# Attention outputs with tokens on partitions, in a fused attention and mixture-of-experts kernel

## The chip, the cores and the metric

One core of a Trainium2 chip runs the whole program. The metric is the device time of one execution in microseconds; lower is better. All arithmetic is float32 (some matmuls of the expert part in a rounded float32 form).

## What is computed

The reference chains three parts: a linear attention with a complex decay for each position and row, a top-1 mixture of experts with a skip test, and a second feed-forward layer. Cut to what matters here:

```python
# q, k, v, a_re, a_im: (B, H, S, D) = (4, 8, 768, 48); a is normalised to magnitude at most 0.999
for t in range(S):
    S_re, S_im = ar * S_re - ai * S_im + k_t v_t^T, ar * S_im + ai * S_re
    y[:, :, t] = q_t^T S_re
x = y as (3072 tokens, 384)                 # heads side by side
skip = x @ w_skip > 0                       # only these tokens are computed
logits = x @ w_gate                         # 8 experts, the largest is taken
x += gate * (relu(x @ w1[e]) @ w2[e])       # on the computed tokens
out = max(x @ m1, x @ m2, x @ m3) @ m_out
```

w_gate and w_skip stand side by side as nine columns ("logits" below means all nine).

## The kernel before

**Two stages.** The attention turns the decays into running products and angles, so that q and k can be scaled and turned beforehand and a step becomes ordinary masked attention within 128 tokens (a chunk) and a state between chunks. Behind it the routing and the experts run; their instructions have line 49 in the profile, since they are issued through a recording helper.

**What sets the order.** Every operation is given to a planner (class Plan) with an engine, an assumed duration and the tiles it reads and writes. The planner walks through time with these durations, always takes the ready operation with the earliest place in the program shifted by a bias, and writes down a fixed order for each engine. The biases are in the table PRIO (by kind of operation and batch). Each engine then runs its order strictly.

**Preparing q and k.** For each batch (the last in two parts, so five units) and each of three groups of 128 rows, ScalarE (line 444) and VectorE (line 476) compute logarithms, angles and their sines in the tiles wa, wCD and wR and multiply q and k (wqk) with them; two scans on VectorE (lines 514 and 560) run along time. The last values of the scans are copied into rhoend and phend (lines 517 and 563, on VectorE). DMAs on SP's queue (line 571, the last unit's second half on GpSimd's) stack the results into qks, where each head has 48 rows of real and 48 of imaginary part; rows 96 to 127 are padding, zeroed by three DMAs (blank, line 325).

**A step** (function step) handles one chunk of one batch for four heads; 48 steps in all. Each half of the heads has its own single buffers, so that its steps follow each other through them:
- line 608: four transposes of k into the bank pk; ScalarE copies them to kn (line 610);
- line 621: scores, eight matmuls in which 64 keys at a time are stationary and the queries stream: 128 columns for the first 64 keys, 64 for the second (their upper triangle is left out). A float32 matmul is two records in the trace, so 16 records. The order alternates heads and halves of the partitions so that two equal widths stand side by side;
- line 624: VectorE multiplies the 256 columns on the diagonal with the mask into pt; line 627: ScalarE copies the other 128 columns;
- line 637: the state z is updated with kn stationary and v streaming in 64 columns; line 642: ScalarE copies it to st;
- line 652: outputs from the state, with st stationary and q streaming in 128 columns;
- line 659: outputs from the scores, v stationary in quarters of 64 x 64 and the scores streaming. v is needed on the other half of the partitions too, so half of it comes a second time in another arrangement (cross, from the array vx, two chunks a load, line 436, two buffers). The outputs stand with head dimensions on partitions;
- line 662: ScalarE copies the outputs to ysb; line 666, the picks: with ysb stationary, the tile w9p (an identity beside the nine weight columns) streams in 105 columns, which turns the outputs to tokens on partitions and appends the nine partial logits; lines 674 and 676: ScalarE copies both to xt and lgw; line 683 sums the logits, line 687 stores x (SP).

SP's queue carries, in one order, the loads of a, q and k (line 421), v (428), cross (436), the stacks (571), the stores of x (687) and later the expert weights. When the tiles of the preparation are no longer used, their memory goes to the expert weights (a mark named swap), whose loads then start.

## Time and profile before

| | us |
|---|---|
| runs: median (lowest to highest of 3) | 677.92 (675.98 to 678.57) |
| profiled execution, device time | 670.54 |
| its span, first to last instruction | 668.8 |
| TensorE busy | 592.6 (89%) |
| VectorE busy | 455.7 (68%) |
| ScalarE busy | 383.0 (57%) |
| GpSimd busy | 62.9 (9%) |

Busy time is the time in which an engine had an instruction running; matmuls overlap each other, so a busy TensorE can still take more work. A row of the timeline or of the chain begins with its start and its length in us. In rows by group, "idle before" is the engine's idle time ahead of these instructions and what ended it.

### The profile page before, as it was taken

How to read it: one execution, taken by the hardware profiler on the slowest of the kernel's cores; microseconds unless marked ns; L12 is line 12 of the kernel's file. 1: busy time of each engine (PE TensorE's matmuls, PEld its weight loads, DVE VectorE, ACT ScalarE, POOL GpSimd, SP SyncE). 2: the span in 40 equal slices, each digit the busy share in tenths (PEclk: the TensorE clock that was granted, in tenths of full speed). 3: DMA queues.
4: the chain of work that ended last, by engine and by line, in shares of the span. 5: the costliest groups of instructions: out<-in, count | busy, mean ns of one | idle time of the engine just before them, and what ended most of it. 6: DMA issues, size and time to landing. Idle time of an engine off the chain costs nothing.

```text
span 668.8 us, 14161 instructions
## 1 busy us (share of the span) xinstructions
PE 592.6 (89%) x5669; PEld 547.0 (82%) x5669; DVE 455.7 (68%) x748; ACT 383.0 (57%) x800; POOL 62.9 (9%) x73
## 2 busy tenths in 40 slices
PE   0008988999999999989999999999999999999996
PEld 0007877889888889979999999899898898998995
DVE  6997999989778766999999854837456464303120
ACT  7797999999967666667677422523324333213120
POOL 1000000000012021030100163204020000000000
PEclk9999999999999999999999999999999999999998
DMA  9979779978749667868884456344042140010000
GB/s 307 301 189 263 291 215 317 289 219 275 210 141 299 223 201 241 307 218 293 274 288 162 156 154 207 99 152 131 1 167 93 32 170 12 13 36 0 25 25 28
DMA packets 60025, 117.40 MB, mean 176 GB/s; under 512 B 6032, under 2 KB 45472, under 8 KB 59952
## 3 DMA queue, kind: packets, MB, share of 16 engines
q1 hardware_dynamic: 51584, 84.57, 40.5%
q10 hardware_dynamic: 4512, 19.66, 8.5%
q0 software_dynamic: 3856, 12.19, 6.2%
q8 instruction: 46, 0.75, 0.5%
q14 instruction: 27, 0.22, 0.1%
HBM read 82.59 MB, written 12.58 MB: 142 GB/s over the span
## 4 chain that ended last, share of the span: by engine, by line
PE 65%; DVE 11%; ACT 11%; DMA 6%; issue 4%; SPq 1%; POOL 0%; ACTq 0%; POOLq 0%; DVEq 0%
PE bank L49 56%; ACT wCD L444 4%; DVE wqk L476 2%; PE bank L659 2%; PE bank L621 2%; DVE wR L476 2%; ACT wa L444 2%; DVE u L49 2%; PE bank L637 1%; DMA w9p<-in_w 1%; DMA wraw<-y_slot,r_grow 1%; PE bank L666 1%; PE bank L652 1%; DMA x<-in_m 1%; ACT kn L610 1%
## 5 line engine op out<-in xcount | busy, mean ns | idle before, releaser
L49 PE MATMUL bank<-ar,wh 128*128 128x512 f32 (+1 forms) x504 | 137.2, 359 | 0.7 <-DVE xs L49 0.7
L49 PEld LDWEIGHTS bank<-ar,wh 128*128 128x128 f32 x504 | 90.0, 189 | 14.9 <-DVE xs L49 1.0
L49 PE MATMUL bank<-ar,wl 128*128 128x512 f32 (+1 forms) x252 | 90.5, 359 | 0.0
L49 DVE TENSOR_TENSOR xs<-bank,xs 128x512 f32<-128x512 f32 (+1 forms) x42 | 25.7, 613 | 69.9 <-PE bank L49 69.7
L608 PE MATMUL bank<-ident,qks 96*128 96x96 f32 x160 | 22.8, 269 | 52.3 <-DMA qks<-wqk 50.8
L49 PE MATMUL bank<-ar,sm 128*128 128x384 f32 x348 | 67.0, 337 | 0.0
L49 PE MATMUL bank<-xth,ar 128*128 128x256 f32 x312 | 63.4, 287 | 3.0 <-DVE sm L49 2.2
L608 PEld LDWEIGHTS bank<-ident,qks 96*128 96x128 f32 x160 | 15.5, 147 | 56.0 <-issue 45.4
L49 PEld LDWEIGHTS bank<-ar,sm 128*128 128x128 f32 x348 | 59.2, 189 | 0.0
L49 DVE TENSOR_TENSOR ar<-wraw,ar 128x768 fp32r<-128x768 f32 x58 | 54.6, 952 | 4.3 <-ACT ar L49 4.0
L49 PEld LDWEIGHTS bank<-xth,ar 128*128 128x128 f32 x312 | 50.9, 190 | 5.1 <-DVE sm L49 3.3
L49 ACT CAST ar<-wraw 128x768 fp32r<-128x768 f32 x58 | 48.2, 834 | 11.4 <-PE bank L49 8.5
L49 PE MATMUL bank<-woh,sm 128*128 128x384 f32 x192 | 53.9, 334 | 0.0
L49 ACT COPY ysb<-bank 128x384 f32<-128x384 f32 x40 | 18.6, 479 | 61.6 <-PE bank L49 61.3
L49 PEld LDWEIGHTS bank<-ar,wl 128*128 128x128 f32 x252 | 47.6, 189 | 6.9
L444 ACT ACTIVATE wCD<-wCD 128x768 f32<-128x768 f32 (+3 forms) x67 | 51.1, 790 | 2.7 <-DVE wCD L514 2.5
L621 PE MATMUL bank<-qks 128*64 128x128 f32 (+1 forms) x768 | 42.4, 254 | 3.2 <-ACT pt L627 1.8
L49 PE MATMUL bank<-xtl,ar 128*128 128x256 f32 x156 | 44.0, 282 | 0.0
L444 ACT ACTIVATE wa<-wa 128x768 f32<-128x768 int32 (+8 forms) x53 | 41.3, 801 | 3.3 <-DVE wa L560 2.3
L49 ACT ACTIVATE wraw<-wraw 128x768 f32<-128x768 f32 x24 | 19.6, 843 | 40.9 <-DVE u L49 35.1
L621 PEld LDWEIGHTS bank<-qks 128*64 128x64 f32 x768 | 38.5, 141 | 5.3 <-ACT pt L627 2.5
L49 PE MATMUL bank<-lnh,ar 128*128 128x384 f32 x144 | 40.9, 337 | 0.0
(223 smaller groups left out, 1411.7 us busy)
## 6 DMA issues: line engine op xcount, KB each, us to landing
wraw<-in_w SPq DMA_DIRECT2D x62, 384.0 KB, 4.8
wraw<-in_a ACTq DMA_DIRECT2D x12, 768.0 KB, 5.4
wqk<-in_qk SPq DMA_DIRECT2D x9, 768.0 KB, 9.5
x<-in_m ACTq DMA_DIRECT2D x9, 768.0 KB, 7.0
qks<-wR SPq DMA_DIRECT2D x18, 288.0 KB, 4.3
qks<-wqk SPq DMA_DIRECT2D x18, 288.0 KB, 5.2
v<-in_v SPq DMA_DIRECT2D x4, 1152.0 KB, 12.1
wa<-in_a SPq DMA_DIRECT2D x6, 768.0 KB, 13.4
```

Of the source, the lines that this page charges most:

```text
L49: return lambda *a, **kw: fn(*map(placed, a), **{n: placed(x) for n, x in kw.items()})
L444: lambda: nc.scalar.activation(out=out[0], in_=in_[0], func=f, **kw), keys(in_), keys(out))
L476: pl.add("DVE", t, lambda: fn(out=out[0], **{m: i[0] for m, i in zip(names, ins)}, **kw), keys(*ins), keys(out), bias=bias)
L608: nc.tensor.transpose(pk[:, h, :2 * D], K[:2 * D, h, sl], ident[:2 * D, :2 * D])
L610: pl.add("ACT", t_acp(384), lambda: nc.scalar.copy(kn[:, 0:8 * D].rearrange("p (h r) -> p h r", r=2 * D), pk[:, :, 0:2 * D]), (pkk,), (knk ...
L621: nc.tensor.matmul(p6[side[o], quads(j, n), :], K[:, 2 * j + o, part[n]], Q[:, 2 * j + o, part[n].start:sl.stop], start=True, stop=True)
L637: nc.tensor.matmul(z[side[o], h * ZW:h * ZW + ZW], kn[:, at:at + HC], vcols(h, ZW), start=c == 0 and h == 0, stop=c == NC - 2 and h == 3, ...
L652: nc.tensor.matmul(py[side[h % 2], h // 2, :], sp[0][:, h * D:h * D + 64], Q[:, h, sl], start=h < 2, stop=False, skip_group_check=True)
L659: nc.tensor.matmul(py[side[o], j, n * HC:], half(j, n, o), t6[side[o], quads(j, n), :], start=c == 0 and j + n == 0, stop=n == 1, skip_gro ...
L666: nc.tensor.matmul(px[side[o], j, :], ysb[:, j, side[o]], w9p[:, 2 * hh + j, :], start=True, stop=True)
```

## The change

The outputs are computed with tokens on partitions at once, so that the turn by the picks is not needed:
- Outputs from the scores: the masked scores are stationary (128 keys x 64 tokens) and v streams. Outputs from the state: q is stationary (64 tokens at a time) and the state streams. Each head streams 57 columns: 48 of v and 9 that hold v times the head's nine weight columns. The picks, ysb and the copy of outputs go; xt and lgw are copied straight from the outputs' bank.
- The nine columns of v: for each chunk the transposed v (array vt, 192 KB a chunk, tile vt with one buffer) is loaded, multiplied with the weights arranged by head (six matmuls of 72 columns, in the bank that also takes the transposes of k), and ScalarE copies the 72 columns into v's wider tile. The state carries the columns too (57 in place of 48).
- Scores: all four heads, one after the other, wide and narrow matmul in turn; the mask is 512 columns wide (128 a head) and the copy of unmasked scores goes. The part of the bank that no matmul writes is zeroed once.
- cross and vx go. The padding of qks is zeroed by GpSimd memsets at the start in place of DMAs.
- The copies to rhoend and phend move from VectorE to ScalarE.
- The table PRIO has new numbers, so the planner's order differs in many places; rows of it stand in the prediction.

```diff
-PRIO = dict(FE=(-150, 400, 200, -200, 400), FT=(400, 400, 100, 10, 200), AE=(10, -100, 60, 150, -200),
+PRIO = dict(FE=(-150, 300, 200, 250, 30), FT=(300, 400, 100, -30, 30), AE=(150, 30, 150, 250, 60), AT=(0, 150, -150, -30, -100),
...
-VW = HD // 2
-VG = 2
-XW = 2 * D + 9
+VW = D + 9
...
-    ring("pt", [P, 6 * HC], NPT)
-    ring("ysb", [P, 2, C], 2)
+    ring("vt", [P, KD, C], 1)
+    ring("pt", [P, 4 * C], NPT)
...
+    for t in qks:
+        nc.gpsimd.memset(t[2 * D:], 0.0)
...
+    def load_vt(b, c):
+        t, k = pl.take("vt")
+        pl.dma(lambda: nc.sync.dma_start(out=t, in_=vt[b, c].rearrange("p (k s) -> p k s", k=KD)), 5 * C * HD, (), (k,),
+               after=stacked.get(b - 1, ()))
+        return t, k
...
-        pl.add("DVE", 75, lambda: nc.vector.tensor_copy(out=rhoend[:, i:i + 1], in_=Dt[0][:, n - 1:n]), keys(Dt), (("rho", i),),
-               bias=PRIO["FE"][now[0]])
+        pl.add("ACT", 190, lambda: nc.scalar.copy(rhoend[:, i:i + 1], Dt[0][:, n - 1:n]), keys(Dt), (("rho", i),))
...
-        pl.add("DVE", 85, lambda: nc.vector.tensor_copy(out=phend[:, i, c0:c1], in_=c3(Bt[0])[:, :, C - 1]), keys(Bt), (("ph", i),),
-               bias=PRIO["FT"][now[0]])
+        pl.add("ACT", 195, lambda: nc.scalar.copy(phend[:, i, c0:c1], c3(Bt[0])[:, :, C - 1]), keys(Bt), (("ph", i),))
...
+        if hh == 0:
+            tv, tvk = load_vt(b, c)
+            lw = pk[:, 8 * D:8 * D + H * 9]
+
+            def f():
+                for k in range(KD):
+                    for o in range(2):
+                        nc.tensor.matmul(lw[side[o]], tv[:, k, side[o]], w9p[:, k, :], start=k == 0, stop=k == KD - 1,
+                                         skip_group_check=True)
+            pl.add("PE", 6 * 63, f, (tvk, "w9p"), (pkk,), form=1)
...
+        if hh == 0:
+            pl.add("ACT", t_acp(72), lambda: nc.scalar.copy(
+                vt[:, c * H * VW:(c + 1) * H * VW].rearrange("p (h w) -> p h w", w=VW)[:, :, D:],
+                lw.rearrange("p (h n) -> p h n", n=9)), (pkk,), vk[1:], bias=PRIO["kn"][b])
...
-            for j, n, o in heads:
-                nc.tensor.matmul(p6[side[o], quads(j, n), :], K[:, 2 * j + o, part[n]], Q[:, 2 * j + o, part[n].start:sl.stop],
-                                 start=True, stop=True)
+            for h in range(4):
+                for n in range(2):
+                    nc.tensor.matmul(p4[side[n], h, n * HC:], K[:, h, part[n]], Q[:, h, part[n].start:sl.stop], start=True, stop=True)
...
-        masked = pl.add("DVE", t_dve(4 * HC) + 10, lambda: nc.vector.tensor_tensor(
-            out=t6[:, 0:4], in0=p6[:, 0:4], in1=mask[:, None, :].to_broadcast([P, 4, HC]), op=ALU.mult), (ppk,), (ptk,),
+        masked = pl.add("DVE", t_dve(4 * C) + 10, lambda: nc.vector.tensor_tensor(
+            out=t4, in0=p4, in1=mask[:, None, :].to_broadcast([P, 4, C]), op=ALU.mult), (ppk,), (ptk,),
             bias=PRIO["mask"][b])
-        pl.add("ACT", t_acp(2 * HC), lambda: nc.scalar.copy(pt[:, 4 * HC:6 * HC], pp[:, 4 * HC:6 * HC]), (ppk,), (free,),
-               after=(masked,), bias=PRIO["free"][b])
...
             for h in range(4):
-                nc.tensor.matmul(py[side[h % 2], h // 2, :], sp[0][:, h * D:h * D + 64], Q[:, h, sl], start=h < 2, stop=False,
-                                 skip_group_check=True)
+                for o in range(2):
+                    nc.tensor.matmul(py[side[o], h, :], Q[:, h, part[o]], sp[0][:, h * VW:(h + 1) * VW], start=h == 0, stop=False,
+                                     skip_group_check=True)
...
-            for j, n, o in heads:
-                nc.tensor.matmul(py[side[o], j, n * HC:], half(j, n, o), t6[side[o], quads(j, n), :],
-                                 start=c == 0 and j + n == 0, stop=n == 1, skip_group_check=True)
-        pl.tail = masked, pl.add("PE", 4 * 165, f, (vk, xk, ptk, free), (pyk, ("px", pyk)), form=2)
-        pl.add("ACT", t_acp(256), lambda: nc.scalar.copy(ysb, py), (pyk,), (ysk,), bias=PRIO["ysb"][b])
-        def f():
-            for j in range(2):
+            for h in range(4):
                 for o in range(2):
-                    nc.tensor.matmul(px[side[o], j, :], ysb[:, j, side[o]], w9p[:, 2 * hh + j, :], start=True, stop=True)
-        pl.add("PE", 4 * 92, f, (ysk, "w9p"), (("px", pyk),), form=1)
+                    nc.tensor.matmul(py[side[o], h, :], t4[:, h, side[o]], vcols(h), start=c == 0 and h == 0, stop=True,
+                                     skip_group_check=True)
+        pl.tail = masked, pl.add("PE", 8 * 64, f, vk + (ptk,), (pyk,), form=1)
```

In the order rows of the changed kernel, line 603 are the scores, 605 the mask, 581 the logits of v, 589 the transposes, 616 the state, 630 and 638 the outputs, 549 the stacks, 416 the loads of vt, 659 the stores of x.

## Rows read from the trace of the kernel before

**Rows 1.** Busy us and instructions by stage; then granted clock, DMA share, GB/s.

```profile
core 0: us, PE busy (x) PEld busy (x) DVE busy (x) ACT busy (x) POOL busy (x), PEclk, DMA share, GB/s
20.00:50.06 30.06, 0.79 (x2) 0.36 (x2) 29.96 (x30) 26.39 (x33) 0.00 (x0) 1.00 0.88 251
50.06:91.00 40.94, 35.58 (x620) 31.55 (x622) 37.19 (x45) 36.04 (x85) 0.00 (x0) 1.00 0.92 275
91.00:140.00 49.00, 44.89 (x872) 39.82 (x870) 46.37 (x55) 47.38 (x118) 0.00 (x0) 1.00 0.84 260
140.00:199.11 59.11, 56.80 (x1146) 51.64 (x1144) 47.18 (x87) 52.95 (x150) 1.54 (x3) 1.00 0.72 216
199.11:224.50 25.39, 23.95 (x449) 21.10 (x446) 20.30 (x47) 17.61 (x48) 6.25 (x10) 1.00 0.89 285
```

**Rows 2.** Chain that ended last: start us, us, what.

```profile
90.79 2.94 ACT wCD L444 x4
...
204.92 5.85 DMA wraw<-in_w
...
404.46 257.63 PE bank L49 x1370
```

**Rows 3.** Timeline: last product with an angle, last sum of logits.

```profile
198.42 0.69 DVE L476 TENSOR_TENSOR wqk<-wqk,wa 128x512 f32<-128x512 f32 x1
...
224.93 0.55 DVE L683 TENSOR_REDUCE lg<-lgw 128x54 f32<-128x216 f32 x1 [0.55 <-ACT lgw L676]
```

**Rows 4.** Chain on TensorE, one stretch of steps: start us, us, records.

```profile
169.84 1.49 PE bank L659 x32
171.33 0.48 PE bank L608 x4
...
172.32 0.67 PE bank L621 x16
172.99 0.47 PE bank L637 x16
173.46 0.44 PE bank L652 x8
173.90 0.36 PE bank L666 x8
```

**Rows 5.** Groups by form, ScalarE: busy us, mean ns; idle before, releaser.

```profile
L662 ACT COPY ysb<-bank 128x256 f32<-128x256 f32 x48 | 17.8, 383 | 6.5 <-PE bank L659 6.3
...
L627 ACT COPY pt<-bank 128x128 f32<-128x128 f32 x48 | 13.2, 283 | 5.2 <-DVE pt L624 4.9
...
L676 ACT COPY lgw<-bank 128x18 f32<-128x18 f32 x48 | 9.4, 203 | 0.0
```

**Rows 6.** The same of VectorE.

```profile
L49 DVE TENSOR_TENSOR xs<-bank,xs 128x512 f32<-128x512 f32 x30 | 20.7, 690 | 60.9 <-PE bank L49 60.7
L624 DVE TENSOR_TENSOR pt<-bank,mask 128x256 f32<-128x256 f32 x48 | 19.6, 418 | 11.4 <-PE bank L659 6.9 <-PE bank L621 4.5
...
L517 DVE COPY rhoend<-wCD 128x1 f32<-128x1 f32 x15 | 2.1, 142 | 0.0
```

**Rows 7.** VectorE's waits, 50 to 230 us (us, times, longest); the longest one.

```profile
DVE pt L624 <- PE bank L659: 6.9, 7, 3.4
DVE pt L624 <- PE bank L621: 4.5, 6, 1.3
DVE wCD L476 <- ACT wCD L444: 2.7, 3, 1.7
...
63.31 0.42 DVE L624 TENSOR_TENSOR pt<-bank,mask 128x256 f32<-128x256 f32 x1 [3.44 <-PE bank L659]
```

**Rows 8.** GpSimd's memset of w9p; loads of cross (ns to issue; us to landing).

```profile
2.47 0.46 POOL L328 MEMSET w9p<- 128x420 f32 x1
...
L436 SPq DMA_DIRECT2D cross<-in_vx x12: 328/539/2938, 17.7 to 194.9; - x12
...
DMA to landing us min/median/max: 2.3/4.6/10.9
```

More of the change, by code (lines that the diff above doesn't have):

```diff
@@ L299, in loaded_rows, with attention @@
     return at
-def attention(tc, ctx, pl, a4, qk4, v, vx, w9, x_dram, lg, ident, phend, rhoend, keep, banks, swap, shift):
+def attention(tc, ctx, pl, a4, qk4, v, vt, w9x, x_dram, lg, ident, phend, rhoend, keep, banks, swap, shift):
     nc = tc.nc
@@ L321, in attention @@
     qks = [(head if i == 2 else const).tile([P, 4, 2, S], F32, name=f"qks{i}") for i in range(NST)]
-    def blank(i):
-        none = pl.slots["st0"][0][2 * D:, 0:S // 4]
-        nc.sync.dma_start(out=qks[i][2 * D:].rearrange("p h a (n s) -> p (h a n) s", n=4),
-                          in_=none[:, None, :].to_broadcast([P - 2 * D, 32, S // 4]))
-    w9p = const.tile([P, 4, XW], F32, name="w9p")
-    nc.gpsimd.memset(w9p, 0.0)
-    for o in range(2):
-        nc.gpsimd.tensor_copy(out=w9p[:, :, o * D:o * D + D],
-                              in_=ident[:, None, 64 * o:64 * o + D].to_broadcast([P, 4, D]))
+    w9p = const.tile([P, KD, H * 9], F32, name="w9p")
     def router():
-        for o in range(2):
-            nc.sync.dma_start(out=w9p[64 * o:64 * o + D, :, 2 * D:], in_=w9.rearrange("(i o e) n -> o e i n", o=2, e=D)[o])
-    lgw = keep.tile([P, 2 * NC, 4, 9], F32, name="lgw")
+        nc.sync.dma_start(out=w9p, in_=w9x)
+    lgw = keep.tile([P, NC, H, 9], F32, name="lgw")
     wide = {}
@@ L427, in load_v @@
         behind = stacked.get(b - 1, ())
-        pl.dma(lambda: nc.sync.dma_start(out=t[:, :NC * HD].rearrange("p (c e) -> p c e", c=NC),
-                                         in_=v[b].rearrange("(c p) e -> p c e", p=C)), 5 * S * HD, (), (k,), after=behind)
-    def load_cross(b, c):
-        if (b, c // VG) not in crosses:
-            t, k = crosses[b, c // VG] = pl.take("cross")
-            cols = slice(c // VG * VG * VW, (c // VG + 1) * VG * VW)
-            pl.dma(lambda: nc.sync.dma_start(out=t[:, :VG * VW], in_=vx[b][:, cols]), 5 * P * VG * VW, (), (k,),
-                   after=stacked.get(b - 1, ()))
-        return crosses[b, c // VG]
+        pl.dma(lambda: nc.sync.dma_start(out=t.rearrange("p (c e) -> p c e", c=NC),
+                                         in_=v[b].rearrange("(c p) e -> p c e", p=C)), 5 * S * HD, (),
+               (k,) + tuple(("vw", k, c) for c in range(NC)), after=behind)
+    def load_vt(b, c):
[3 more added lines that the diff above has]
+        return t, k
     c3 = lambda t: t.rearrange("p (c s) -> p c s", s=C)
@@ L588, in step @@
         vt, vk = T[b, "v"]
-        vcols = lambda h, w=64, rows=slice(0, P): vt[rows, c * HD + (4 * hh + h) * D:c * HD + (4 * hh + h) * D + w]
+        vk = (vk, ("vw", vk, c))
+        vcols = lambda h: vt[:, (c * H + 4 * hh + h) * VW:(c * H + 4 * hh + h + 1) * VW]
         part = slice(c * C, c * C + HC), slice(c * C + HC, c * C + C)
         side = slice(0, HC), slice(HC, P)
-        xv, xk = load_cross(b, c)
-        heads = [(j, n, o) for j in range(2) for n in range(2) for o in range(2)]
-        quads = lambda j, n: slice(2 * j + 1, 2 * j + 2) if n else every(2 * j, 4 - j, 2)
-        def half(j, n, o):
-            if n == o:
-                return vcols(2 * j + o, 64, side[o])
-            at = c % VG * VW + (2 * hh + j) * D
-            return xv[side[o], at:at + 64]
-        last = c == NC - 1
+        last = c == NC - 1
+        if not last or hh == 0:
+            pk, pkk = pl.take("pk")
+        if hh == 0:
[7 more added lines that the diff above has]
+            pl.add("PE", 6 * 63, f, (tvk, "w9p"), (pkk,), form=1)
         if not last:
-            pk, pkk = pl.take("pk")
             kn, knk = pl.take("kn")
@@ L709, in attention @@
             pl.dma(router, 60000, (), ("w9p",), 900)
-            for j in range(2):
-                pl.dma(lambda j=j: blank(j), 1572864, (), (("blank", j),), 900 - 300 * j)
-        if i == 1:
-            pl.dma(lambda: blank(2), 1572864, (), (("blank", 2),), after=stacked[0])
         use_set("natural_log_exp_and_others")
@@ L1700, in general, with fused @@
             last(tc, ctx, x2_dram, m_w, m_out, out, ident)
-def fused(tc, a4, qk4, v, vx, w9, w1, w2, m1, m2, m3, mo, out):
+def fused(tc, a4, qk4, v, vt, w9, w9x, w1, w2, m1, m2, m3, mo, out):
     nc = tc.nc
@@ L1731, in shift @@
                 next_sb.open()
-            swapped, shifted, rooms = attention(tc, (outer, middle, front), pl, a4, qk4, v, vx, w9, x_dram, lg, ident, phend, rhoend, const,
+            swapped, shifted, rooms = attention(tc, (outer, middle, front), pl, a4, qk4, v, vt, w9x, x_dram, lg, ident, phend, rhoend, const,
                                                 banks, swap, shift)
```

94 lines of the change are left out of this document (44 added, 50 removed).

## Prediction

> **What bounds the kernel now.** I read the busy table by stage first, then the chain of work that ended last, then the pace of single groups, then what VectorE waits for. Before 50 us TensorE does almost nothing; from 404 us on the chain is TensorE alone, in one piece of 257.6 us [rows 2]. The change touches neither part: its work lies between, in the 48 attention steps (4 batches, 2 halves of the heads, 6 chunks of 128 tokens), which run from about 50 to 224.5 us [rows 1, 3]. So the question is by how much the end of that stage moves; the expert work behind it stands in the same order in both kernels and should move as a block.
>
> In that stage no engine is alone at its limit [rows 1]. From 50 to 140 us ScalarE is busy 83.4 of 90 us and VectorE 83.6 of 90, and the chain runs through long pieces of ScalarE, as four activations without a gap at 90.79 [rows 2]. From 140 to 199 TensorE is busy 56.8 of 59.1 us, with VectorE at 47.2 and ScalarE at 53.0. What closes the stage is VectorE's last product with an angle, at 198.42 to 199.11 [rows 3]: it frees the buffers for the expert weights and gives the last q and k to TensorE. Then TensorE finishes the steps that are left, and the last sum of logits at 224.93 opens the second routing.
>
> **TensorE's part.** In the stretch that TensorE bounds, one step costs [rows 4], from start to start: transposes 0.48 us, scores 0.67 (16 records), state update 0.47 (16 records of 64 columns), outputs from the state 0.44 (8 records of 128), outputs from the scores 1.49 for two steps, so 0.745, and picks 0.36: 3.165 us. The records show a price per column: 16 x 64 = 1024 columns in 0.47, 8 x 128 = 1024 in 0.44, 16 x 96 = 1536 in 0.67, so about 0.44 ns a column while the two halves of the partitions alternate with equal widths. With it the new step: picks gone (-0.36). Outputs from the scores become 16 records of 57 columns: 912 columns, 0.40 by columns, 0.47 if 57 cost what 64 cost; I take 0.43, so -0.315. State and state outputs the same way 0.43 each, -0.04 and -0.01. The scores keep their 16 records, but a wide one (128) on one half of the partitions now always follows a narrow one (64) on the other, so the halves no longer balance: the wide half alone is 8 x 128 columns at twice 0.44, 0.90 us, +0.23. At the low end they balance after all (0). The logits are 12 records of 72 columns per two steps, 0.38, so +0.19 a step. Sum: -0.36 - 0.315 - 0.05 + 0.23 + 0.19 = -0.305 us a step, **14.6 us** less over 48 steps (12 to 26 by the bounds).
>
> The Trainium skill, "TensorEngine Tiling (Array Packing)", section "Instruction Overhead", gives each matmul about 60 cycles of overhead and advises not to take a tiling factor from a dimension that is already small. By it 57 columns cost what 60 do, so the 16 records would take 0.42 us in place of 0.40; the row of 64 columns agrees as far as it goes, and the value taken lies above both.
>
> **ScalarE's part.** A copy of the unmasked scores (283 ns) and the copy of outputs for the picks (383 ns) go from each step [rows 5]: 48 x 0.666 = 32.0 us. Added: 24 copies of 72 logits at about 0.22 us (the 18-wide one takes 203 ns), 5.3; wider state and logit copies, about 2.2; and the 30 small copies of scan ends that leave VectorE, at the same 0.2, 6.0. Net **-18.5 us**.
>
> **VectorE's part** goes the other way. The mask now takes 512 columns, not 256: the row for a TENSOR_TENSOR of 512 columns out of PSUM has 690 ns against the mask's 418 [rows 6], +13.1 us over 48. The 30 small copies go, at 142 ns [rows 6], -4.3. So VectorE gets **8.8 us** more in a stage where two thirds of the time already find it at 93% or more. What counts is what stands ahead of its last product. VectorE's order there, before:
>
> ```order
> L624 TENSOR_TENSOR pt_161<-bank_110,mask 128x256
> L476 SCALAR_TENSOR_TENSOR wCD<-wR,wCD 128x256
> L476 TENSOR_SCALAR wa<-wa 128x256
> L476 TENSOR_TENSOR wqk<-wqk,wCD 128x2x256
> L624 TENSOR_TENSOR pt_160<-bank_109,mask 128x256
> L476 TENSOR_TENSOR wR<-wqk,wa 128x2x256 x2
> L476 TENSOR_TENSOR wqk<-wqk,wa 128x2x256 x2
> L624 TENSOR_TENSOR pt_161<-bank_110,mask 128x256
> L476 TENSOR_TENSOR wR<-wqk,wa 128x2x256
> L476 TENSOR_TENSOR wqk<-wqk,wa 128x2x256
> ```
>
> and in the changed kernel at the same place (the last rows ahead of the first routing):
>
> ```order
> L655 TENSOR_REDUCE lg<-lgw 128x54
> L605 TENSOR_TENSOR pt_153<-bank_110,mask 128x512
> L539 SCALAR_TENSOR_TENSOR wa<-wa,phend,zero_126 128x256 x2
> L456 TENSOR_TENSOR wqk<-wqk,wCD 128x2x256
> L456 TENSOR_SCALAR wa<-wa 128x2x256
> L456 TENSOR_TENSOR wqk<-wqk,wCD 128x2x256
> L456 TENSOR_SCALAR wa<-wa 128x256
> L456 TENSOR_TENSOR wqk<-wqk,wCD 128x2x256
> L605 TENSOR_TENSOR pt_152<-bank_109,mask 128x512
> L605 TENSOR_TENSOR pt_153<-bank_110,mask 128x512
> L456 TENSOR_TENSOR wR<-wqk,wa 128x2x256 x3
> L456 TENSOR_TENSOR wqk<-wqk,wa 128x2x256 x3
> ```
>
> Counted down the whole order, 42 of the 48 masks stand ahead of the last product before, 40 after. So from 50.06 us (where batch 0's products end in both, after the same amount of VectorE work) VectorE has 40 x 0.690 - 42 x 0.418 = +10.0 us of masks and 24 copies less, -3.4: **+6.6 us**. Its busy time there is 37.2 + 46.4 + 47.2 = 130.7 of 149.05 us [rows 1], so 18.3 us are idle, and the change gains only if more than 6.6 of them go. Masks waited for TensorE 6.9 + 4.5 us and VectorE for ScalarE's activations 2.7 [rows 7] (about 2.5 of the first sum lie behind 199 us). The 3.44 us of one mask, at 63.3 us, go: in the new order a scan stands ahead of that place and work is ready. TensorE and ScalarE have 9% and 11% less to do, so I take two thirds of what is left of the waits: idle falls from 18.3 to 8, and the last product comes at 199.1 + 6.6 - 10.3 = **195.4**, 3.7 us earlier. If the idle time stays it comes at 205.7; if it falls to 3, at 190.4.
>
> **Behind the last product** 8 masks are left in place of 6, two more steps for TensorE (+5.7), and the other seven are 0.31 cheaper (-2.2); TensorE is busy 23.95 of 25.4 us there [rows 1], so +3.5. The last step's way to its logits is shorter: the copy before the picks (0.38), the picks (0.36) and the copy of unmasked scores (0.28) go, the outputs from the scores lose 0.3, the mask and the scores gain 0.27 and 0.23: -0.8 [rows 4 to 6]. Together +2.7. Added to -3.7 that is -1.0; but the extra steps partly fill time in which the stage waits for the first expert weights (5.85 us on the chain, [rows 2]), so I count half of the 2.7: **-2.4 us**.
>
> **Loads and start.** The three copies of zeros over the padding (768 KB each) go to GpSimd as three memsets of 6144 elements. Its memset of 420 took 0.46 us [rows 8], so each is at most 6.7 us, 20 in all, over by 26 us; nothing reads the padding before the first scores, after 50 us [rows 1], which hides them. Without that cover, up to 20 us. On TensorE's first scores the new order puts one more scaling and one more pair of VectorE operations ahead of the second group's product, some 2 us later; TensorE is not the bound there, so nothing.
>
> The new loads of transposed v are 24 of 192 KB in one buffer, against 12 of 192 KB in two. They stand on SP's queue between the stacks of q and k, and each waits for the logits of the chunk before. SP, before and after, at batch 1's first stacks:
>
> ```order
> L687 DMA x_dram<-xt_164 128x384
> L436 DMA cross_144<-in_vx 128x384
> L687 DMA x_dram<-xt_165 128x384
> L571 DMA qks_130<-wR 48x1536 x2
> L571 DMA qks_130<-wR 32x1536
> L571 DMA qks_130<-wqk 48x1536 x2
> L571 DMA qks_130<-wqk 32x1536
> ```
>
> ```order
> L659 DMA x_dram<-xt_154 128x384
> L659 DMA x_dram<-xt_155 128x384
> L416 DMA vt_139<-in_vt 128x384
> L549 DMA qks_130<-wR 48x1536 x2
> L549 DMA qks_130<-wR 32x1536
> L549 DMA qks_130<-wqk 48x1536 x2
> L549 DMA qks_130<-wqk 32x1536
> L416 DMA vt_139<-in_vt 128x384
> ```
>
> A load that waits now holds the stacks behind it. On TensorE two groups of logits can stand close together, as early in batch 0:
>
> ```order
> L581 MATMUL bank_107<-w9p,vt_139 64x72 x6
> L589 MATMUL bank_107<-ident,qks_128 128x96 x4
> L616 MATMUL bank_113<-v_137,kn_148 64x57 x8
> L638 MATMUL bank_111<-v_137,pt_152 64x57 x8
> L616 MATMUL bank_114<-v_137,kn_149 64x57 x8
> L638 MATMUL bank_112<-v_137,pt_153 64x57 x8
> L581 MATMUL bank_107<-w9p,vt_139 64x72 x6
> ```
>
> That is 2.6 us of matmuls between two uses of one buffer, by the prices above; such a load took 0.54 us to issue and 4.6 to land [rows 8]. Thirteen of the gaps are shorter than 5.1 us, short by 13.7 us in all. As long as TensorE has its 14.6 us to spare and the real gaps are stretched by waits for masks, I count it at 0; the bound is 13.7.
>
> **The sum.** The profiled execution took 670.54 us (span 668.8); the runs' median is 677.92, 1.1% more. On its own time the forecast is 668.1; on the runs' scale **675.5**, less than the 0.5% (3.4 us) that a measurement of this kernel can tell from no change.
>
> **Rivals.**
> - *TensorE was the bound and its saving counts in full.* For it: 56.8 of 59.1 us busy from 140 on, and the chain there. Against: VectorE has only 18.3 us to give. Then the stage ends 12 to 17 us earlier: 661 to 666.
> - *VectorE's idle time doesn't shrink.* Its waits are for a fixed order, and each mask still waits for its own scores through single buffers. Then the last product comes 6.6 us later and the tail adds 2: 685. It decides as soon as fewer than 6.6 of 18.3 idle us go.
> - *The single buffer of transposed v.* TensorE stands at the logits until the load lands, masks come late, SP holds the stacks. If half of the 13.7 us stand on the path beside the forecast's gain: 680 to 685, slower. It decides if TensorE waits at logits for more than about 6 us. For it: 13 gaps; against: loads of this size landed in 2.3 us at best [rows 8].
> - *Nothing moves*: what goes was hidden and the engines trade waits: 678.
>
> **How the numbers follow.** Forecast (670 to 679) 0.42, TensorE in full 0.20, VectorE's idle time stays 0.15, the buffer 0.18, nothing 0.05. The forecast's case gives half its chance to faster and half to same: faster 0.20 + 0.21 and a little of the buffer's case at its light end, 0.43; same 0.21 + 0.05 + 0.04 = 0.30; slower 0.27. The range reaches from TensorE in full to VectorE in full, 662 to 686; where signs are mixed, the forecast's own range is 670 to 679.
>
> **What would show it.** Masks at about 0.69 us; scores at about 0.9 us for 16 records, outputs from the scores at about 0.43; TensorE's busy time between 60 and 200 us well under 90%; VectorE over 94% there, with its last product near 195 us; the last sum of logits near 222; the same distance from it to the end as before (444 us). Wrong it would be if TensorE waits for the load of transposed v (its idle time ahead of the logits), if the last product comes after 200 us, or if the part behind 243 us changes length.

## The result and the profile after the change

The changed kernel is slower: 685.97 us median (682.7 to 688.7) against 676.95 for the kernel before, a ratio of 1.014 with a 95% interval of 1.011 to 1.017. The forecast was 675.5. The profiled execution of the changed kernel is its longest one (688.7 us, span 687.0), that of the kernel before (670.5) is shorter than all four of its runs here (675.8 to 678.6), so the two traces overstate the difference. A second pair of traces, both from one chip, has spans of 681.0 and 672.6; it is used below where the size matters.

Busy time by stage in the changed kernel, with the columns of [rows 1], cut at the new ends of the stages:

```profile
50.06:91.00 40.94, 31.87 (x606) 29.21 (x607) 38.09 (x37) 35.02 (x75) 0.00 (x0) 0.96 0.89 281
91.00:140.00 49.00, 41.51 (x876) 37.31 (x875) 46.22 (x46) 43.79 (x101) 0.00 (x0) 0.93 0.76 249
140.00:207.42 67.42, 56.40 (x1207) 51.24 (x1205) 54.46 (x76) 45.60 (x129) 0.45 (x1) 0.90 0.74 218
207.42:238.80 31.38, 27.80 (x624) 25.55 (x619) 24.27 (x53) 19.46 (x54) 7.79 (x12) 1.00 0.84 261
```

VectorE is busy 138.8 us between 50.06 us and its last product (38.09 + 46.22 + 54.46), 8.0 more than before, and idle for 18.6 of 157.4: as much as before (18.3). (In the second trace it is idle for 14.2 us, before 18.5.) TensorE's granted clock is 0.96, 0.93 and 0.90 up to that product; before, each stage had 1.00.

In the timeline, beside [rows 3], the last product ends at 207.46 (before 199.11), the last sum of logits at 238.86 (225.48).

```profile
205.57 1.89 DVE L456 TENSOR_TENSOR wqk<-wqk,wa 128x512 f32<-128x512 f32 x3
...
237.88 0.98 DVE L655 TENSOR_REDUCE lg<-lgw 128x54 f32<-128x432 f32 x1
```

So the stage loses 8.3 us ahead of the product and 5.0 behind it (31.4 us from product to sum, before 26.4); from the sum to the end it is 448.1 us against 443.3. On the pair from one chip it is 4.1 and 5.6 (203.6 to 235.9, against 199.5 to 226.2), and the distance from there to the end is 445.1 against 446.4. So on that pair all of the loss lies in the attention stage; the 4.8 us behind it in the first pair are no more than this distance varies among the traces below (442 to 451 us).

The chain of work that ended last (start us, us, what, as in [rows 2]): loads of transposed v now stand on it.

```profile
148.72 7.15 DMA vt<-in_vt
...
187.30 4.49 DMA vt<-in_vt
...
212.39 4.66 DMA vt<-in_vt
219.05 5.88 DMA vt<-in_vt
...
420.98 260.31 PE bank L49 x1370
```

The waits between 50 and 245 us (us, times, longest) name the same thing at the logits, L581. The masks (L605) wait longer than in [rows 7], and the state update (L616) waits for ScalarE's copy of the logit columns into v (L593).

```profile
PEld bank L581 <- DMA vt<-in_vt: 14.6, 7, 4.0
PE bank L581 <- DMA vt<-in_vt: 13.2, 7, 3.8
DVE pt L605 <- PE bank L638: 11.2, 6, 5.0
...
DVE pt L605 <- PE bank L603: 7.9, 8, 1.6
...
PE bank L616 <- ACT v L593: 6.7, 6, 3.1
```

One of the waits at the logits, in TensorE's timeline, and the stretches around it (columns as in [rows 1]):

```profile
155.91 0.99 PE L581 MATMUL bank<-w9p,vt 128*64 128x72 f32 x12 [3.75 <-DMA vt<-in_vt]
...
162.03 0.90 PE L589 MATMUL bank<-ident,qks 96*128 96x96 f32 x4
162.87 1.11 PE L630 MATMUL bank<-st,qks 128*64 128x57 f32 x16
...
166.72 0.55 PE L589 MATMUL bank<-ident,qks 96*128 96x96 f32 x4
167.20 0.68 PE L630 MATMUL bank<-st,qks 128*64 128x57 f32 x16
```

```profile
152.00:156.00 4.00, 0.25 (x4) 0.09 (x4) 3.93 (x6) 3.63 (x5) 0.00 (x0) 0.73 1.03 241
156.00:160.00 4.00, 3.31 (x46) 2.87 (x48) 2.22 (x2) 1.55 (x6) 0.00 (x0) 0.50 1.03 311
160.00:164.00 4.00, 4.00 (x49) 3.44 (x46) 2.54 (x4) 1.95 (x7) 0.00 (x0) 0.50 1.06 380
164.00:168.00 4.00, 4.00 (x95) 3.72 (x94) 2.92 (x6) 3.09 (x9) 0.00 (x0) 0.99 0.95 324
```

TensorE stands for 3.75 us; then the granted clock is 0.50 (1.2 of 2.4 GHz) for 8 us, in which it gets through 95 records (46 and 49), as many as in the 4 us behind them. From the start of four transposes to the next group it takes 0.84 us there (162.03 to 162.87) and 0.48 at full clock (166.72 to 167.20). The Trainium skill describes this in "TensorE: Matmul & The Clock Gate", section "HAM oscillation — how this bites in real kernels": a wait for a DMA in each tile makes the tile behind it start at half clock, and the loop should be laid out so that TensorE does not wait. The trace agrees.

The load is not the only new wait. In the changed kernel v's tile is complete for a chunk only when ScalarE has copied the 72 logit columns into it, and in ScalarE's fixed order that copy can stand behind long activations of the preparation. One case, in TensorE's timeline:

```profile
80.87 0.68 PE L616 MATMUL bank<-v,kn 128*64 128x57 f32 x16 [3.12 <-ACT v L593]
```

Behind this pause, too, the granted clock is near half (0.55 and 0.60 from 82 to 86 us).

### The profile page after: what moved, and what is told of

It reads as the page before. It is cut to its first block, busy times and chain, and to the rows that moved or that the text cites. A ratio compares the mean times of both kernels' runs of the same rounds, so it can differ in the third digit from the quotient of the medians.

```text
span 687.0 us, 14519 instructions
## 1 busy us (share of the span) xinstructions
PE 591.1 (86%) x5893; PEld 547.7 (80%) x5893; DVE 468.3 (68%) x720; ACT 372.2 (54%) x758; POOL 79.6 (12%) x68
## 4 chain that ended last, share of the span: by engine, by line
PE 65%; DVE 11%; DMA 10%; ACT 7%; issue 5%; SPq 1%; another core or an unknown queue 0%; POOL 0%; ACTq 0%; POOLq 0%; DVEq 0%
PE bank L49 55%; DMA vt<-in_vt 4%; PE bank L603 3%; ACT wCD L424 2%; ACT wa L424 2%; DVE wR L456 2%; DVE wqk L456 2%; PE bank L589 1%; PE bank L616 1%; PE bank L630 1%; DVE u L49 1%; PE bank L638 1%; DMA x<-in_m 1%; DVE wCD L494 1%; PE bank L581 1%
## 5 line engine op out<-in xcount | busy, mean ns | idle before, releaser
L603 PE MATMUL bank<-qks 128*64 128x128 f32 (+1 forms) x768 | 56.4, 271 | 31.8 <-DMA qks<-wqk 30.3
L603 PEld LDWEIGHTS bank<-qks 128*64 128x64 f32 x768 | 45.6, 147 | 35.0 <-issue 31.5
L49 ACT COPY ysb<-bank 128x384 f32<-128x384 f32 x40 | 18.6, 480 | 63.5 <-PE bank L49 63.2
L605 DVE TENSOR_TENSOR pt<-bank,mask 128x512 f32<-128x512 f32 x48 | 32.4, 686 | 19.1 <-PE bank L638 11.2
L581 PE MATMUL bank<-w9p,vt 128*64 128x72 f32 x288 | 16.4, 252 | 33.3 <-DMA vt<-in_vt 33.3
L581 PEld LDWEIGHTS bank<-w9p,vt 128*64 128x64 f32 x288 | 13.2, 155 | 35.0 <-issue 20.0
```

Source lines behind the costliest of these rows:

```text
L49: return lambda *a, **kw: fn(*map(placed, a), **{n: placed(x) for n, x in kw.items()})
L581: nc.tensor.matmul(lw[side[o]], tv[:, k, side[o]], w9p[:, k, :], start=k == 0, stop=k == KD - 1, skip_group_check=True)
L603: nc.tensor.matmul(p4[side[n], h, n * HC:], K[:, h, part[n]], Q[:, h, part[n].start:sl.stop], start=True, stop=True)
L605: masked = pl.add("DVE", t_dve(4 * C) + 10, lambda: nc.vector.tensor_tensor(out=t4, in0=p4, in1=mask[:, None, :].to_broadcast([P, 4, C]), ...
```

## The experiments

Each ratio is to the kernel before on the same chip; its median there was 670 to 676 us. "Last product", "idle" (VectorE's idle time from 50.06 us to that product) and "tail" (from it to the end of the last sum of logits) are read from each trace as above, in us. The two traces of the changed kernel differ by 3.9 us in the last product, so a difference of that size between two single traces decides nothing.

| kernel | ratio, 95% interval | last product | idle | tail |
|---|---|---|---|---|
| before, second trace (b0) | 1 | 199.5 | 18.5 | 26.7 |
| changed, second trace (a0) | 1.015 (1.010 to 1.019) | 203.6 | 14.2 | 32.3 |
| e1 second buffer | 1.017 (1.010 to 1.023) | 206.8 | 17.7 | 31.0 |
| e2 one load | 1.005 (1.003 to 1.007) | 198.0 | 9.4 | 31.8 |
| e3 half masks | 1.011 (1.006 to 1.017) | 200.5 | 21.0 | 30.8 |
| e4 both | none | 197.0 | 17.6 | 31.2 |
| e5 second buffer, GpSimd's queue | 1.014 (1.011 to 1.017) | 202.6 | 13.2 | 33.8 |
| e6 one buffer, GpSimd's queue | 1.011 (1.008 to 1.014) | 199.2 | 9.9 | 32.7 |
| e7 masks split | 1.051 (1.047 to 1.054) | 219.9 | 32.7 | 40.8 |
| e8 transposes twice | 1.021 (1.018 to 1.023) | 210.3 | 20.5 | 32.3 |
| e10 wider masks in the kernel before | 1.001 (0.998 to 1.003) | 201.6 | 15.6 | 26.2 |
| f1 planned, old priorities | 1.002 (0.999 to 1.005) | 200.7 | 12.5 | 28.5 |
| e9 planned, new priorities | 0.999 (0.997 to 1.002) | 197.7 | 9.3 | 25.4 |
| f2 new priorities alone | 1.012 (1.006 to 1.019) | 203.1 | 13.2 | 31.6 |
| f4 planned, SP's queue | 0.997 (0.994 to 1.001) | 199.8 | 10.3 | 25.6 |
| f3 as e9, sines apart | 0.999 (0.995 to 1.002) | 198.5 | 8.8 | 26.2 |
| g1 planned, one buffer | 1.025 (1.022 to 1.028) | 209.3 | 19.2 | 30.0 |
| g2 as f4, sines apart | 0.997 (0.996 to 0.999) | 196.6 | 7.1 | 25.4 |

**Second traces (b0, a0).**

> The kernel before once more, for a trace from the chip of this set: the profile read so far is of an execution of 670.5 us, while the median of its other runs was 676. If the difference is the chip and lies in the expert block, VectorE's last angle product is at 199 us again; if the attention block varies by itself, the product moves by more than 1 us.

> The changed kernel once more, on the same chip as the three others of this set: 1.011 to 1.017 of the kernel before, the last product 7 to 10 us after that of the kernel before on this chip.

Measured: the kernel before has its last product 0.4 us later than in the first trace and the rest of its extra 3.8 us of span behind it, mostly in the expert block; the changed kernel came out as before, with its product 4.1 us behind, less than expected.

**The loads or the masks (e1 to e4).** e1 gives odd chunks a tile of their own and leaves planner and order as they are (the mask moves to another tile, to make room):

```diff
+        if b < B - 1 and c % 2:
+            t = vt1
+        elif b == B - 1 and c:
+            t = pl.slots["v"][0][:, c * HD:(c + 1) * HD].rearrange("p (k s) -> p k s", k=KD)
```

> The changed kernel with more buffers for transposed v: odd chunks of the first three batches get a second tile, and the last three chunks of the last batch go into the tile of v that the third batch has left free. The order of every engine and queue stays as it is. Theory A (the single buffer: a load can be issued only behind the logits of the chunk before, lands 4 to 7 us later, TensorE stands still for it 13 us in all between 50 and 245 us and then runs at half clock): nearly all of these waits go, the granted clock is back at 0.97 or more between 100 and 200 us, VectorE's last angle product comes at 199 to 203 us instead of 207.5, and the time is 674 to 681 us. Theory B (VectorE's masks, 8.8 us more work ahead of the last product, set the time and the waits at the logits only fill what TensorE would have idled anyway): waits go, but masks still end late, last product 206 us or later, time 684 to 688 us.

e2 drops the loads behind the first (`get` issues the load as before):

```diff
-        pl.dma(lambda: nc.sync.dma_start(out=t, ...
+        pl.dma(None if b or c else get, 5 * C * HD, (), (k,), after=stacked.get(b - 1, ()))
```

> The changed kernel with 23 of the 24 loads of transposed v left out: the logits of all chunks read the first chunk's, so the router's choices and the output are not the reference's; every TensorE, VectorE and ScalarE instruction stays. The limit of theory A: no wait for a transposed load, and 4.5 MB less traffic. Theory A: 670 to 679 us, last product at 196 to 202 us, granted clock 0.97 or more up to 200 us. Theory B: 683 to 687 us. If it is more than 3 us below the kernel with two buffers, the rest of the cost is the traffic or the loads' place in SP's queue rather than the buffer.

e3 masks two of four heads (the other half of pt is zeroed once, at the start):

```diff
-            out=t4, in0=p4, in1=mask[:, None, :].to_broadcast([P, 4, C]), op=ALU.mult), (ppk,), (ptk,),
+            out=t4[:, 0:2], in0=p4[:, 0:2], in1=mask[:, None, :].to_broadcast([P, 2, C]), op=ALU.mult), (ppk,), (ptk,),
```

> The changed kernel with the masks on two of the four heads of a step alone, 256 columns instead of 512 (the other half of the weights is zero, so the outputs of half the heads lack what comes from their own chunk): some 0.27 us less for each of 48 masks, 13 us of VectorE in all and 11 us ahead of its last product, which is more than the change added there. The waits for transposed v stay. Theory A: the waits at the logits stay near 13 us, last product at 203 to 207 us, time 681 to 686 us. Theory B: last product at 197 to 201 us, time 674 to 679 us.

e4 is e2 and e3 together.

> Both: one load of transposed v, and masks on two of four heads (logits and half of the outputs are not the reference's). Theory A: as with one load alone, 668 to 677 us, at most 3 us below it. Theory B: as with the half masks alone, 673 to 679 us. If both causes cost by themselves, it is lower than either by 5 us or more: 662 to 668 us.

e2 takes VectorE's idle time from 18.6 us (14.2 in the second trace) to 9.4 with its work unchanged, which fits theory A, as do its time and its last product; the clock does not come back as far as expected (0.95, not 0.97). Its wrong logits send tokens to other experts, but from the last sum of logits to the end it takes 444.9 us, the changed kernel 445.1, so its time can be compared. From 50.06 us to its last product:

```profile
50.06:198.03 147.97, 125.16 (x2681) 114.29 (x2683) 138.54 (x156) 123.97 (x303) 0.51 (x1) 0.95 0.73 233
```

With the loads gone, TensorE's waits for ScalarE's copy at the state update grow from 6.7 to 12.5 us: its three longest pauses behind 52 us (3.15, 4.11 and 3.38 us) are all there, and a stretch at half clock stands behind each. So a part of the wait at the logits only moves one step on. The chain through the first of them (columns as in [rows 2]):

```profile
75.94 0.41 PE bank L581 x10
76.35 0.49 PE bank L589 x4
76.87 0.48 ACT kn L591
77.34 0.78 ACT wa L424
78.15 1.67 ACT wa L424 x2
79.82 0.12 ACT v L593
79.98 0.68 PE bank L616 x16
```

The logits are done at 76.4 us, but three activations stand ahead of their copy. In the other two pauses the copy to kn, which the kernel before has too, is late with it.

e3 takes 9.3 us of work away and the product comes 7 us earlier than in the first trace, 3 than in the second. That product (200.5) lies in theory B's range and the time just below theory A's; the interval overlaps that of the changed kernel, so by time it tells little. In e4 the product is only 1.0 us ahead of e2: without the late loads, less mask work hardly counts. (e4's wrong logits sent it through the kernel's general path behind attention, 17,221 us in all; only its attention stage is read.) But e1, the direct test, did nothing, against theory A's number. Its waits at the logits are 11.1 us in place of 13.2:

```profile
PE bank L586 <- DMA vt<-in_vt: 8.4, 4, 3.2
...
PE bank L586 <- DMA v<-in_vt: 2.7, 2, 1.8
```

and SP's queue, which no longer waits for logits ahead of these loads, waits instead ahead of the stores of x that stand in front of them in its order (36.3 us for lgw, 29.7 in the changed kernel):

```profile
SPq L664 <- ACT lgw L653: 36.3, 10, 8.3
SPq L664 <- ACT v L598: 9.0, 4, 5.8
```

The load that the changed kernel issues at 148.72 us, e1 issues at 149.49. Here the second buffer is of no use to a load whose place in the queue was planned for one.

**The queue (e5, e6).**

```diff
-        pl.dma(lambda: nc.sync.dma_start(out=t, in_=vt[b, c]...
+        pl.dma(lambda: nc.gpsimd.dma_start(out=t, in_=vt[b, c]...
```

> The changed kernel with the two buffers for transposed v and, besides, its 24 loads issued from GpSimd's queue, which has nothing to do from 25 to 180 us, instead of SP's, where they stood behind stacks and stores of x that wait for ScalarE. TensorE's, VectorE's and ScalarE's order stays. Theory A2 (not the buffer but the load's place in SP's queue made the waits: two buffers alone left 11 of the 13 us): the waits at the logits fall below 3 us between 50 and 245 us, VectorE's last product comes at 198 to 201 us as with one load alone, and the time is 677 to 681 us. Theory A3 (the loads' traffic on the DMA engines makes the waits, by delaying them and the stacks): the waits at the logits go or not, but the last product stays at 204 us or later and the time at 683 us or more.

> The changed kernel with a single buffer for transposed v, its loads issued from GpSimd's queue, where they wait for the logits of the chunk before and nothing else, and SP's queue is free of that wait. If the place in SP's queue alone was the cause: 677 to 681 us, as with two buffers on that queue. If buffer and place each make a load late by themselves, only both together help: 683 to 687 us, with 8 us or more of waits at the logits.

e5 fulfils the first half of A2 (2.8 us of waits at the logits are left) and misses the second: its product comes at 202.6 us, its tail is 33.8, and its ratio does not move. (680.6 us lies in the range only because the kernel before takes 670.5 on this chip.) As in e2, TensorE now waits at the state update for ScalarE's copy, 12.9 us in place of 6.7. e6, with 5.5 us of waits left at the logits, fits neither case: its ratio is 0.3% below that of the changed kernel, which the intervals do not tell apart, and its tail is again 32.7. So loads that arrive in time are not enough in an order that was planned without them. Against the second trace of the changed kernel the last product comes 1 us earlier in e5, 4 in e6 and 6 in e2, and the tail stays in all three: a second loss.

**Splitting the masks (e7).** ScalarE copies and GpSimd masks the first 64 queries, VectorE the others.

> Two buffers and GpSimd's queue for transposed v, and the masks cut in two for the first three batches: VectorE takes the 256 columns of the second 64 queries, ScalarE copies the 64x256 of the first 64 queries out of PSUM and GpSimd masks that copy in SBUF. VectorE has 0.27 us less for each of 36 masks (9.7 us), ScalarE 36 copies of some 0.27 us more, GpSimd 36 products of some 0.6 us. If VectorE's masks are what is left once the loads are early, the last product comes 3 to 7 us before that of the kernel with early loads alone and the time is 672 to 678 us; if ScalarE and TensorE are as near as the kernel with one load and half masks suggests (its last product came 1 us before that of one load alone), it is 676 to 681 us; if GpSimd's products slow VectorE or hold the outputs, 681 us or more.

The third case, and worse than it said: GpSimd's product of 64x256 took 1.10 us where 0.6 was expected, ScalarE's copy 0.37. VectorE waits 13.4 us for these copies, and TensorE for copies and products (2.4 and 1.0 us). The loads of transposed v now stand among the products in GpSimd's queue, and 8.7 us of waits are back at the logits, so this run does not test the split by itself.

```profile
L617 POOL TENSOR_TENSOR pt<-pt,k_tmp 64x256 f32<-64x256 f32 x36 | 39.5, 1099 | 138.6 <-ACT pt L615 131.0 <-PE bank L655 4.6 <-PE bank L647 3.0
```

**More work for TensorE (e8)**: `for h in (0, 1, 2, 3) * 2` in the transposes.

> The changed kernel with every transpose of the keys done twice into the same place: 160 more of TensorE's transposes, 0.47 us for each of 40 steps, some 19 us, nothing else. Before the change TensorE's clock was granted in full while it was busy 44 to 48 of each 50 us; after it, busy 41 of 50, it was granted 0.86 to 0.97 of it. If TensorE's time is not what sets the pace, and a part of what it loses to the clock comes back when it is busier: 684 to 691 us, clock up between 100 and 200 us. If TensorE sets the pace: 695 to 705 us.

The time is in the first range but the ratio rises by 0.6% (some 4 us). The added work was 14.6 us by the line's busy time (36.7 against 22.1), not 19, so under a third of it counts. The clock was 0.90 and 0.93 between 100 and 200 us (0.93 and 0.86 to 0.90 in the two traces without the extra work): no better on the whole, against what was expected. In this trace, too, its stretches at half clock stand behind pauses of 3.1 to 3.4 us (before 81.9, 110.3 and 159.7 us).

**VectorE's work alone (e10)**, in the kernel before:

```diff
-            out=t6[:, 0:4], in0=p6[:, 0:4], in1=mask[:, None, :].to_broadcast([P, 4, HC]), op=ALU.mult), (ppk,), (ptk,),
+            out=t6[:, 0:6], in0=p6[:, 0:6], in1=mask[:, None, :].to_broadcast([P, 6, HC]), op=ALU.mult), (ppk,), (ptk,),
```

> The kernel before with each mask widened from 256 to 384 columns (the third part is then overwritten by ScalarE's copy as before, so nothing else changes): by the two widths on record (418 ns for 256, 690 for 512) 0.137 us for each of 48 masks, 6.5 us of VectorE in all and 5.7 us ahead of its last product, near the 6.6 us that the change added there; nothing of the change itself. Theory V (VectorE's 18 us of idle time there are held by chains that its own work runs through, so added work moves the end by nearly its full length): last product 4 to 6 us later, time 4 to 6 us longer (1.006 to 1.009). Theory A (idle time absorbs it, as was forecast, and only late loads lengthen it): last product at most 2 us later, time within 2 us (0.998 to 1.003).

Theory A by the time, which can't be told from no change; the product comes 2.1 us later, at the edge of its range. 5.0 us more work stand ahead of the product (135.96 against 130.94 in b0), of which 3 went into idle time. The change itself added 8.0 us there, so this run covers five eighths of it.

```profile
50.06:201.60 151.54, 137.78 (x2630) 123.13 (x2632) 135.96 (x184) 137.38 (x352) 1.68 (x3) 1.00 0.81 243
```

**Telling the planner (e9, f1, f2, f4, f3).** The planner's own price for one load of transposed v is 650 + 0.0026 x 245,760 + 900 ns, 2.2 us from issue to landing, where loads of that size landed in 4.6 [rows 8] (behind 60 us the medians by stage are 3.1 to 4.4). e9, f1, f4, f3 plan both buffers and 3.0 in place of the 0.9 us, 4.3 in all:

```diff
+        if b < B - 1:
+            t, k = (vt1, ("vt", 1)) if c % 2 else pl.take("vt")
+        elif c == 0:
+            t, k = pl.take("vt")
+        else:
+            t, k = pl.slots["v"][0][:, c * HD:(c + 1) * HD]..., ("vt3", c)
+            free = tuple(pl.readers[("v", 0)])
...
+               after=stacked.get(b - 1, ()) + free, dur=VT[0], eng="POOL", lat=VT[1])
```

f1 does that alone; it is e5 with another plan. e9 has a new table of priorities too; f4 is e9 with `nc.sync` and `dur=625`, f3 is e9 with `trig=(1, 1, 1, 1, 1)`, each with a table of its own; f2 is the changed kernel with a new table and nothing else.

> The changed kernel with two buffers for transposed v and its loads on GpSimd's queue, this time known to the planner (issue and landing time of the loads by the trace, 1.0 and 3.6 us, and both buffers), and the table of priorities set anew for it, so the order of all engines differs. If what is left of the loss is order (the tail of 8 steps behind the last product, 31 to 33 us against 26.4 before): tail 28 us or less and time 0.995 to 1.004 of the kernel before. If it is the masks' work, which no order removes: 1.004 to 1.010.

> Two buffers, GpSimd's queue, and a planner that knows both and the loads' time, but with the changed kernel's own priorities, so the order moves only as far as the loads move it. Theory P (the plan did not know the loads; told of them, any priorities will do): 0.997 to 1.003 of the kernel before. Theory O (the order of the tail is the larger half, and it hangs on the priorities): 1.004 to 1.012, tail behind the last product still 30 us or more.

> The changed kernel with nothing but its table of priorities set anew: single buffer, SP's queue, and a planner that counts a load of transposed v as landing 2 us after its issue. Theory O: 1.000 to 1.006, tail 28 us or less, whatever waits for transposed v are left. Theory P: 1.008 to 1.017, with waits at the logits of 8 us or more between 50 and 245 us.

> Two buffers and planned loads with priorities set for them, but the loads on SP's queue, where the change had them. If the queue only mattered because the plan misplaced the loads in it: 0.996 to 1.003, waits at the logits below 4 us. If loads on SP's queue are late behind stacks and stores of x wherever a plan puts them: 1.005 to 1.014, waits at the logits 8 us or more.

> The kernel with two buffers, planned loads on GpSimd's queue and new priorities, once more with one setting different: the sines of the last unit are taken for one group of 128 at a time and not for three at once, so its products and stacks can start earlier; priorities set for that. 0.993 to 1.002 of the kernel before; if the three-wide sines were worth having, 1.002 to 1.006.

Theory P. f1 brings back 1.2 of the 1.4% with the old priorities, on the buffers and the queue with which e5 stayed at 1.014; f2 brings at most a little with new ones and late loads (7.7 us of waits at the logits, just under theory P's 8); theory O would have had it the other way round. In f1 TensorE waits 2.0 us for ScalarE's copy, in e5 12.9, so the new plan places the copy as well as the load. Which part of what the planner was told does it, the second buffer or the landing time, is open: no run tells it of the buffer with the old price. On SP's queue nothing is lost once the load is planned (f4). The tail shrinks to 28.5 us by planning and to 25.4 with new priorities, though between f1 and e9 the times aren't told apart, and f3 is not told apart from e9.

**One buffer, planned (g1), and the best version (g2).**

> The changed kernel with its single buffer of transposed v and the loads on SP's queue, but a planner that counts 4 us from issue to landing and priorities set for that. If the plan's knowledge is all: 0.998 to 1.005. If one buffer cannot be hidden (24 loads that each can only be issued behind the logits of the chunk before and land 4 to 7 us later), an honest plan only moves the waits from TensorE's queue to the order of the steps: 1.008 to 1.025.

> Two buffers, planned loads on SP's queue, the sines of the last unit one group at a time, priorities set for that: 0.993 to 1.000 of the kernel before. Masks and 8.8 us more of VectorE's work stay, so no more than that.

g1 is the slowest but e7: with an honest price for the load, one buffer makes the plan hold the steps back (only 3.1 us of waits are left at the logits, but VectorE is idle for 19.2 us). So in these runs both are needed, the buffer and a plan that knows it. g2 is faster than the kernel before by 0.1 to 0.4%: 669.2 against 671.2 us. New priorities and single sines were not tried on the kernel before, so this gain isn't shown to be the change's own. TensorE never waits for transposed v there behind 50 us, and SP issues these loads ahead in rows:

```profile
184.25 1.47 SPq L424 DMA_DIRECT2D v<-in_vt  x3
...
186.41 0.59 SPq L424 DMA_DIRECT2D v<-in_vt  x1
```

```profile
50.06:196.56 146.50, 127.20 (x2757) 117.42 (x2759) 139.44 (x158) 127.40 (x317) 3.03 (x6) 0.93 0.85 268
```

The Trainium skill asks for double buffers in "Trainium Kernel Development and Optimization", section "Best Practices", to overlap loads with work. The runs agree only in part: the second buffer by itself gave 1.017, with its loads on a free queue 1.014 (e5), and in an order planned for it 1.002 to 0.997 (f1, e9, f4, g2).

## Why the prediction was wrong, point by point

- **The step that failed** is the load of transposed v, "I count it at 0; the bound is 13.7". TensorE stood 13.2 us at the logits (10.7 in the second trace), near the bound, although it had time to spare. It had it in sum, not where it was needed: TensorE takes its instructions in order, so behind a late load stand the scores for the next mask, and what it does next runs at half clock. Leaving out the loads gives back 0.9% of the 1.4 (e2); two buffers in an order planned for them give back 1.2 with the old priorities (f1) and all of it with new ones (e9, f4). The prediction held the two facts, a load that lands in 4.6 us and 13 gaps shorter than that, and let TensorE's spare sum outweigh them. The single buffer was among the rivals, with its point of decision (6 us of waits) and 680 to 685 us, at 0.18.
- **VectorE's idle time**, "falls from 18.3 to 8", followed from it: it stayed at 18.6 (14.2 in the second trace), so the rival of the unchanged idle time gave nearly the place of the last product (205.7; 207.5 and 203.6 measured). A fixed order by itself does not hold the idle time up: in the same order, without the loads, it is 9.4 (e2). The 8 was also summed too low: it counts the 2.5 us of waits that the prediction itself puts behind 199 us; without them two thirds of the rest give 9.4 and a last product at 196.8. VectorE's added work was 8.0 us, not 6.6: the three sums of logits got wider as well (0.98 against 0.55 us for the last).
- **The tail**, "half of the 2.7", was 5.0 to 5.6 us. That no part hid behind the weights' load can be said; why it is twice the sum was not isolated. It goes with the order: all kernels in the changed order have 8 masks left behind the product and tails of 31 to 34 us (10 masks and 40.8 in e7), f1 has 7 and 28.5, and e9, f4, f3 and g2 have 6, as the kernel before, and 25.4 to 26.2, near its 26.4. The number of masks is not all: f2 has 6 left too, but late loads, and a tail of 31.6.
- **Masks** (686 ns; 690 expected) and **scores** (1.81 us on the chain for the 32 records of two steps, so 0.90 for 16) were right. **Outputs** were mis-sized: 16 records of 57 columns cost 0.47 us, what 64 columns cost in [rows 4], and not 0.43; in a stretch of e2 at full clock:

```profile
93.97 0.47 PE bank L638 x16
94.44 0.47 PE bank L616 x16
94.91 0.47 PE bank L638 x16
95.37 0.38 PE bank L581 x12
95.76 0.46 PE bank L630 x16
```

With these TensorE saves 0.19 us a step, 9 us in all (picks -0.36, outputs from scores -0.275, scores +0.23, logits +0.19, state outputs +0.02), not 14.6, and less than the 12 of the bounds, which leave the two state terms at the price by column. Little of it shows: TensorE's whole busy time fell by 1.5 us (592.6 to 591.1), with a granted clock of 0.92 in place of 1.00 up to the last product.
- **Memsets** of the padding were hidden, at 5.2 us each. **ScalarE** lost what was expected (19.1 us by the sum of its groups, 18.5 forecast). But the new copy of logit columns was priced by its length alone (0.22 us; 0.24 measured) and not as a link between logits and state update: TensorE waited 6.7 us for it, and 12.5 where the loads did not delay it first (e2). No run moves this copy alone, so its share of the loss is not known.
- **The end of the range**, 686, held the time by chance: it came from VectorE's idle time staying in full, with 2 us more of tail, and the time got there by a last product 4 to 8 us later and a tail longer by 5.

g2 measures 2.0 us less than the kernel before, where the sum said 2.4. That is luck as far as the runs show: g2 has a second buffer and another order, and TensorE's term, VectorE's added work and the tail were each off.

## What to carry to other kernels

Where a change puts a new load under a planner, compare the planner's price for it with the landing time of its like in the trace, and list the gaps between uses of its buffer that are shorter; spare time of the engine that waits doesn't cover them, since it waits in order. Follow what the load feeds to its end, too: here a copy of 0.24 us on a third engine, behind that engine's long activations, took over much of the wait when the load was on time. A second buffer counted only once the order of all engines was planned for it, not by a freer queue alone. And test "engine X got more work" by giving the old kernel that work alone (e10): here 5 us of it cost nothing that the time can show.

## What was not expected of the hardware

- After a wait of 3.75 us for a load TensorE's granted clock was 0.50 for 8 us, and after one of 3.12 us for ScalarE it was 0.55 and 0.60 for 4; the kernel before had 1.00 throughout the stage. Even g2, with no wait for transposed v and no single pause over 1.9 us behind 53 us, has 0.93.
- Scores of alternating widths, 128 columns on one half of the partitions and 64 on the other, cost 0.90 us for 16 records against 0.67 for 16 balanced ones [rows 4].
- GpSimd's product of 64x256 in SBUF took 1.10 us; VectorE's mask of 128x256 out of PSUM takes 0.42.
